# Loading two scalars first on two queues, a mask made as one minimum, and a scheduler that counts the first loads' landing

## The chip, the cores and the metric

The kernel runs on one core of one Trainium2 chip. Times are microseconds (us) of device time for one execution; the number quoted for the kernel before, 606.26 us, is the median of 3 runs (606.16 to 608.05). A core has five engines that run side by side: PE (TensorE, matrix products), DVE (VectorE), ACT (ScalarE), POOL (GpSimd) and SP (SyncE, which here only issues DMAs). Each engine executes its own instructions strictly in the order in which they were written for it. DMAs are issued from SP and from ACT; each of the two has its own DMA queue (q1 and q10 in the profile).

## The reference, cut to what matters

```python
B, H, S, D = 2, 8, 768, 64                      # attention; n_global = 8, n_local = 96 are inputs
scores = q @ k.T / sqrt(D)
keep  = (pos_k < n_global) | ((rel >= 0) & (rel < n_local))      # rel = pos_q - pos_k
dist  = where(is_global & ~is_local, n_local, abs(rel))
scores = where(keep, scores - slope[h] * dist, -1e9)
x = softmax(scores) @ v                                           # (1536, 512) over heads
x = silu(x @ w1_in) @ w1_out                                      # 512 -> 2048 -> 512
out = leaky_relu(x @ w2_in) @ w2_out                              # 512 -> 2048 -> 512
```

Only a band of 96 keys, and the first few global keys, enter a row of scores. n_global and n_local are 64-bit integers in DRAM and are known only when the kernel runs, so the mask is made on the chip.

## The kernel before, in words

**Attention.** It is cut into 24 units: two batches, three stretches of 256 queries, four pairs of heads. Unit by unit, PE transposes q and k (`pt`, line 936), ACT or DVE copies them out (`kT`, line 222 or 224, and `qT`, line 951; DVE also copies the global keys beside each block, line 948), PE makes scores (`s`, line 979), DVE adds the mask and takes the row minimum in one instruction (line 1012), ACT takes the exponential (1019), DVE divides (1035), PE transposes the result (`pa`, 1052), and PE multiplies with v (`pv`, 1078). Every unit reads the mask, first `mask0`, then `mask`.

**Mask.** `load_n` (line 77) issues two DMAs on SP that spread n_global and n_local to 128 partitions (`nraw`). DVE turns the 64-bit integers into floats (`masks_n`, 827). POOL makes the column part from n_global (`masks_global`, 834, two instructions), DVE makes the band part (`masks_local`, 838), and DVE joins them (`masks_both`, 842).

**The two layers.** The weights are read as 64-bit floats, and DVE and ACT turn them into pairs of 32-bit parts (`st`, `f`, `wi`, `wo`, lines 264 to 288). PE then does the first layer's products (`ph`, 600), the second's (`po`, 655) and, in later parts, products of sums (`pq`, 490). The products of the first layer are mixed between the units of attention: they are what PE has to do while DVE and ACT work on scores.

**Warm-up.** `warm_up` puts 27 products of zeros (`wps`, 878) into PE's order: 8 before anything else, 3 around the first two units, 16 more at a late priority.

**The order.** `Sched` (120) is a list scheduler that runs when the kernel is built. Each task has an engine, a duration, a priority and its dependences; the scheduler plays through the kernel with these durations and writes each engine's instructions in the order in which they would start. A DMA's landing is put at `max(end, dma) + 1.7` (191). The order is fixed; on the chip each engine waits at an instruction until what it needs is there. The DMAs share eight completion semaphores in turn, so the ninth DMA that is written waits, on its issuing engine, until the first has landed, the tenth until the second, and so on.

Of the kernel before, what the change touches and what calls it, by code (L numbers as in the profile page):

```python
# [9 lines left out]
F32 = mybir.dt.float32  # L10
F32R = mybir.dt.float32r
I32 = mybir.dt.int32
AF = mybir.ActivationFunctionType
ALU = mybir.AluOpType
PSUM = bass.MemoryType.PSUM

P = 128
# [4 lines left out]
BIG = float(2.0 ** 41)  # L22
# [4 lines left out]
def kernel(  # L27
# [23 lines left out]
    nc = tc.nc  # L51
# [14 lines left out]
    const = ctx.enter_context(tc.tile_pool(name="const", bufs=1))  # L66
# [4 lines left out]
    warm = const.tile([P, 1], F32, name="warm")  # L71
# [5 lines left out]
    def load_n(eng):  # L77
        for x, src in enumerate((n_global, n_local)):
            eng.dma_start(out=nraw[:, x], in_=src.bitcast(I32).partition_broadcast(P))
# [5 lines left out]
    m8nl = const.tile([P, 1], F32, name="m8nl")  # L85

# [33 lines left out]
    class Sched:  # L120
# [19 lines left out]
        def run(self):  # L140
# [3 lines left out]
            for t in self.tasks:  # L144
                for e in t["eng"]:
                    free.setdefault(e, 0.0)
                    ready.setdefault(e, [])
                for b in t["bufs"]:
                    if b.tile is not None and not b.held:
                        b.held = True  # L150
                        used[b.key] = used.get(b.key, 0) + 1
            seq, dma = 0, 0.0
# [12 lines left out]
            while len(order) < len(self.tasks):  # L165
                for e in free:
# [22 lines left out]
                    if t["dma"]:  # L189
                        dma = max(dma, now + 0.4) + t["land"]  # L190
                        end = max(end, dma) + 1.7
                    else:
                        end += t["land"]
# [591 lines left out]
    with ExitStack() as es:  # L785
# [28 lines left out]
        m8rel, pen, col = mk[:, 0:256], mk[:, 256:512], mk[:, 512:640]  # L814
        nc.gpsimd.iota(
            m8rel[:, P:256], pattern=[[8, P]], base=0, channel_multiplier=-8, allow_small_or_imprecise_dtypes=True
        )
        nc.gpsimd.affine_select(
# [5 lines left out]
        )  # L824
        nc.gpsimd.iota(col, pattern=[[1, P]], base=0, channel_multiplier=0, allow_small_or_imprecise_dtypes=True)

        def masks_n():
            nc.vector.tensor_copy(npair, nraw)
            nc.vector.tensor_scalar(nhi, npair[:, :, 0], 0.0, None, op0=ALU.is_lt)
            nc.vector.tensor_tensor(nhi, nhi, npair[:, :, 1], op=ALU.add)  # L830
            nc.vector.scalar_tensor_tensor(nf, nhi, float(2.0 ** 32), npair[:, :, 0], op0=ALU.mult, op1=ALU.add)
            nc.vector.tensor_scalar(m8nl, nlf, -8.0, None, op0=ALU.mult)

        def masks_global(eng):
            eng.tensor_scalar(col, col, ngf, -BIG, op0=ALU.is_ge, op1=ALU.mult)
            eng.tensor_scalar(col, col, m8nl, 0.0, op0=ALU.add, op1=ALU.add)

        def masks_local():
            nc.vector.tensor_scalar(pen, m8rel, m8nl, -BIG, op0=ALU.is_le, op1=ALU.mult)
            nc.vector.tensor_tensor(mask, m8rel, pen, op=ALU.add)  # L840

        def masks_both():
            nc.vector.tensor_copy(mask[:, NPV:P], col[:, 0:NG])
            nc.vector.tensor_tensor(mask0, mask[:, P:256], col, op=ALU.max)

        masks = (masks_n, masks_global, masks_local, masks_both)
# [13 lines left out]
        nload = add("SP", 0.9, lambda eng: load_n(eng), -13.0, (), (), land=0.1)  # L860
        add("ACT", 1.4, lambda eng: eng.activation(warm, warm, AF.Exp), -9.0, (), (), at=2.0)
        mt = add("DVE", 0.95, lambda eng: masks[0](), -0.5, (nload,), (), at=3.9)
        mp = add("POOL", 0.9, lambda eng: masks[1](eng), -0.5, (mt,), ())
        mt = add("DVE", 0.75, lambda eng: masks[2](), -0.5, (mt,), ())
        mtask = add("DVE", 0.45, lambda eng: masks[3](), -0.5, (mt, mp), ())
# [400 lines left out]
```

## Time and profile before

| | us |
|---|---|
| median of 3 runs | 606.26 |
| the profiled execution, its own time | 607.96 |
| its span, from the first to the last instruction | 606.2 |
| PE busy | 596.1 |
| DVE busy | 528.4 |
| ACT busy | 305.4 |

The profile tells of one execution. Its span (606.2) is what the views cut into pieces; the 1.8 us between the span and that execution's own time lie outside the views. Engine time is "busy" when an instruction stands on the engine; a line of the wait view says how long an engine sat idle and which event ended that. For DMAs the issue (how long the issuing engine is held) and the landing (from issue to the last byte's completion) are two numbers.

### The profile page before, as it was taken

The page shows a single profiled execution, that of the slowest core. Times are in us where ns is not written, and L with a number is a line of the kernel's source. Part 1 is how long each engine was busy: PE and PEld are TensorE (multiplying, and loading weights), DVE is VectorE, ACT ScalarE, POOL GpSimd, SP SyncE. Part 2 cuts the span into 40 slices and gives each one's busy share as a digit, 9 for nine tenths or more (in the row PEclk, how much of TensorE's full clock was granted, in tenths as well). Part 3 has the DMA queues.
Part 4 walks back from the last instruction along what each step waited for, and adds up shares of the span by engine and source line. Part 5 has one row for each costly group of instructions (what it writes and reads, how often), then busy time and mean ns, then how long its engine had stood idle before and what let it go on. Part 6 is the DMA issues. An engine that isn't in the chain of part 4 may idle for free.

```text
span 606.2 us, 9115 instructions
## 1 busy us (share of the span) xinstructions
PE 596.1 (98%) x3266; PEld 490.0 (81%) x3267; DVE 528.4 (87%) x1213; ACT 305.4 (50%) x682; POOL 3.7 (1%) x20
## 2 busy tenths in 40 slices
PE   8999999999999999999999999999999999999996
PEld 4678777778888888888888888898898889888985
DVE  4999999877999999995999999899999997978551
ACT  4789887876654435432555554556343433333110
POOL 2000000000000000000000000000000000000000
PEclk9999999999999999999999999999999999999999
DMA  8875568310012332322231111322132322010112
GB/s 180 185 174 141 136 167 203 71 36 1 0 36 70 105 105 69 106 69 70 69 105 35 36 35 36 105 69 85 54 105 71 104 70 69 6 65 1 70 55 90
DMA packets 72676, 49.43 MB, mean 82 GB/s; under 512 B 50480, under 2 KB 67120, under 8 KB 72624
## 3 DMA queue, kind: packets, MB, share of 16 engines
q1 hardware_dynamic: 71536, 48.51, 28.6%
q8 instruction: 28, 0.46, 0.3%
q10 hardware_dynamic: 1088, 0.26, 0.2%
q14 instruction: 24, 0.20, 0.1%
HBM read 45.62 MB, written 3.15 MB: 80 GB/s over the span
## 4 chain that ended last, share of the span: by engine, by line
PE 94%; DVE 3%; DMA 2%; ACT 1%; issue 0%; ACTq 0%
PE po L655 43%; PE pq L490 29%; PE ph L600 10%; PE s L979 3%; PE pa L1052 3%; PE pv L1078 3%; PE pt L936 2%; DMA st<-in_moe_w_in_dram 1%; DVE A L1012 1%; PE wps L878 1%; DMA q<-in_q_dram 1%; DVE A L1035 0%; DMA k<-in_k_dram 0%; ACT AT L222 0%; ACT A L1019 0%; DVE f L279 0%
## 5 line engine op out<-in xcount | busy, mean ns | idle before, releaser
L655 PE MATMUL po<-g,wo 128*128 128x512 f32 x576 | 141.5, 392 | 0.0
L655 PE MATMUL po<-wo,g 128*128 128x512 f32 (+1 forms) x588 | 136.2, 385 | 0.0
L655 PEld LDWEIGHTS po<-wo,g 128*128 128x128 f32 x588 | 107.7, 188 | 21.0
L655 PEld LDWEIGHTS po<-g,wo 128*128 128x128 f32 x576 | 106.9, 188 | 21.7 <-DVE wo L288 0.2
L600 PE MATMUL ph<-x,wi 128*128 128x512 f32 (+1 forms) x336 | 77.6, 366 | 0.9 <-DVE wi L288 0.6
L505 DVE TENSOR_TENSOR tl<-tl,pq 128x512 f32<-128x512 f32 (+1 forms) x110 | 64.3, 585 | 10.3 <-PE pq L490 5.3
L600 PEld LDWEIGHTS ph<-x,wi 128*128 128x128 f32 x336 | 56.4, 188 | 11.0 <-DVE wi L288 1.2
L490 PE MATMUL pq<-xs,ws 128*128 128x512 f32 x252 | 62.3, 389 | 0.0
L490 PEld LDWEIGHTS pq<-xs,ws 128*128 128x128 f32 x252 | 47.3, 188 | 9.8
L273 ACT ACTIVATE st<-st 128x512 f32<-128x512 f32 x64 | 42.9, 670 | 23.5 <-DMA st<-in_moe_w_out_dram 13.2
L1019 ACT ACTIVATE A<-A,nm 128x256 f32<-128x256 f32 (+1 forms) x96 | 46.1, 483 | 12.1 <-DVE nm L1012 11.9
L687 DVE SCALAR_TENSOR_TENSOR yp<-po,yp 128x512 f32<-128x512 f32 x60 | 40.7, 686 | 9.4 <-PE po L655 9.1
L279 DVE SCALAR_TENSOR_TENSOR f<-st,f 128x512 int32<-128x512 int32 x64 | 43.9, 687 | 0.9
L282 DVE SCALAR_TENSOR_TENSOR f<-st,f 128x512 int32<-128x512 int32 x64 | 43.8, 684 | 0.4
L575 ACT ACTIVATE g<-tl 128x512 fp32r<-128x512 f32 x40 | 25.0, 630 | 37.5 <-DVE tl L570 29.0
L490 PE MATMUL pq<-xn,wi 128*128 128x512 f32 (+1 forms) x192 | 43.1, 336 | 0.0
L1012 DVE CUSTOM_DVE_ANT_0 A<-s,mask 128x256 f32<-128x256 f32 (+1 forms) x96 | 34.7, 393 | 3.9 <-PE s L979 3.7
L222 ACT ACTIVATE wo<-f 128x512 fp32r<-128x512 f32 x30 | 18.9, 630 | 34.6 <-PE po L655 17.2
L490 PEld LDWEIGHTS pq<-xn,wi 128*128 128x128 f32 x192 | 32.3, 189 | 4.5
L578 DVE TENSOR_TENSOR g<-tl,g 128x512 fp32r<-128x512 f32 x40 | 27.1, 686 | 5.1 <-ACT g L575 4.8
L575 ACT ACTIVATE g<-t 128x512 fp32r<-128x512 f32 x32 | 20.1, 630 | 19.7 <-PE po L655 10.8
L276 DVE TENSOR_SCALAR f<-st 128x512 int32<-128x512 int32 x64 | 26.7, 420 | 1.6 <-ACT st L273 1.6
(119 smaller groups left out, 883.2 us busy)
## 6 DMA issues: line engine op xcount, KB each, us to landing
st<-in_moe_w_in_dram SPq DMA_DIRECT2D x32, 512.0 KB, 3.8
st<-in_moe_w_out_dram SPq DMA_DIRECT2D x32, 512.0 KB, 3.6
vd<-in_v_dram SPq DMA_DIRECT2D x24, 128.0 KB, 2.8
q<-in_q_dram SPq DMA_DIRECT2D x22, 128.0 KB, 3.1
k<-in_k_dram SPq DMA_DIRECT2D x22, 128.0 KB, 3.4
out_dram<-yo SPq DMA_DIRECT2D x11, 256.0 KB, 2.1
vp<-in_v_dram SPq DMA_DIRECT2D x20, 96.0 KB, 2.7
vp<-in_v_dram SPq DMA_DIRECT2D x20, 32.0 KB, 2.4
```

The costliest lines, as they stand in the source:

```text
L273: eng.activation(hf, hf, AF.Copy, scale=2.0 ** -112)
L279: eng.scalar_tensor_tensor(fi(), lo(), 29, fi(), op0=ALU.logical_shift_right, op1=ALU.bitwise_or)
L282: eng.scalar_tensor_tensor(fi(), hi(), -(2 ** 31), fi(), op0=ALU.bitwise_and, op1=ALU.bitwise_or)
L490: eng.matmul(bank[c]()[:, :w], wt_()[:, a, f0:f0 + P], x()[:, b, c0:c0 + w], start=(first and kk == 0 and i == 0), stop=(kk == 1 and i == ...
L505: eng.tensor_tensor(dst[0]()[:, dst[1]], a[0]()[:, a[1]], b[0]()[:, b[1]], op=op)
L575: eng.activation(g()[:, 0, :], t(), AF.Copy)
L578: eng.tensor_tensor(g()[:, 1, :], t(), g()[:, 0, :].bitcast(F32), op=ALU.subtract)
L600: eng.matmul(ph()[:, :w], wv[:, a, kk, :], xs[kk]()[:, b, cs], start=(kk == 0 and i == 0), stop=(kk == NKK - 1 and i == 2),)
L655: eng.matmul(po()[:, :w], lhsT, rhs, start=(j == 0 and i == 0), stop=(j == FPP - 1 and i == 2))
L687: eng.scalar_tensor_tensor(dst()[:, cs], po()[:, :w], scale, y()[:, cs], op0=ALU.mult, op1=ALU.add)
L1012: eng.tensor_tensor_reduce(A()[:, i, j, c0:256], s[j]()[:, i, c0:256], mask0 if c0 else mask, -QSCALE * SLOPE[2 * hp + j], 3.0e38, ALU.add ...
L1019: eng.activation(a, a, AF.Exp, bias=nm()[:, x:x + 1], scale=-1.0, accum_out=su()[:, x:x + 1])
```

## The change

Three things change. The two scalars are loaded by the first DMA of ACT's queue (n_global) and the first of SP's (n_local), ahead of all q and k; before, both stood on SP behind the first two q loads. The mask is made from tables of distances that POOL prepares without n (three new instructions on POOL, in place of the two that waited for n); what depends on n is then four DVE instructions on the tables in place of four on DVE and two on POOL, and `masks_n` keeps five. And the scheduler starts SP and ACT at 0.75, and puts a DMA's landing at the later of 2.4 after its issue and 1.7 after its turn on the DMA engines; with other numbers the whole order of the program is found anew.

```diff
-    def load_n(eng):
-        for x, src in enumerate((n_global, n_local)):
-            eng.dma_start(out=nraw[:, x], in_=src.bitcast(I32).partition_broadcast(P))
+    def load_n(eng, x):
+        eng.dma_start(out=nraw[:, x], in_=(n_global, n_local)[x].bitcast(I32).partition_broadcast(P))
...
-                    free.setdefault(e, 0.0)
+                    free.setdefault(e, 0.75 if e in ("SP", "ACT") else 0.0)
...
-                        end = max(end, dma) + 1.7
+                        end = max(end + 2.4, dma + 1.7)
...
+        nc.gpsimd.tensor_scalar(far[:, P:256], m8rel[:, P:256], BIG / 4, -BIG, op0=ALU.mult, op1=ALU.add)
...
+        nc.gpsimd.tensor_scalar(far[:, 0:P], m8rel[:, 0:P], BIG / 4, -BIG, op0=ALU.mult, op1=ALU.add)
...
+        nc.gpsimd.tensor_scalar(col, col, -2 * BIG, -BIG, op0=ALU.mult, op1=ALU.add)
...
-            nc.vector.tensor_scalar(nhi, npair[:, :, 0], 0.0, None, op0=ALU.is_lt)
-            nc.vector.tensor_tensor(nhi, nhi, npair[:, :, 1], op=ALU.add)
+            nc.vector.scalar_tensor_tensor(nhi, npair[:, :, 0], 0.0, npair[:, :, 1], op0=ALU.is_lt, op1=ALU.add)
...
-        def masks_global(eng):
-            eng.tensor_scalar(col, col, ngf, -BIG, op0=ALU.is_ge, op1=ALU.mult)
-            eng.tensor_scalar(col, col, m8nl, 0.0, op0=ALU.add, op1=ALU.add)
+            nc.vector.tensor_scalar(nfar, nf, 2 * BIG, None, op0=ALU.mult)
...
-            nc.vector.tensor_scalar(pen, m8rel, m8nl, -BIG, op0=ALU.is_le, op1=ALU.mult)
-            nc.vector.tensor_tensor(mask, m8rel, pen, op=ALU.add)
+            nc.vector.scalar_tensor_tensor(mask, far, nfar[:, 1:2], m8rel, op0=ALU.add, op1=ALU.min)
...
-        def masks_both():
+        def masks_global():
+            nc.vector.tensor_scalar(col, col, nfar[:, 0:1], m8nl, op0=ALU.add, op1=ALU.min)
+            nc.vector.tensor_tensor(mask0, mask[:, P:256], col, op=ALU.max)
             nc.vector.tensor_copy(mask[:, NPV:P], col[:, 0:NG])
-            nc.vector.tensor_tensor(mask0, mask[:, P:256], col, op=ALU.max)
...
-        nload = add("SP", 0.9, lambda eng: load_n(eng), -13.0, (), (), land=0.1)
-        add("ACT", 1.4, lambda eng: eng.activation(warm, warm, AF.Exp), -9.0, (), (), at=2.0)
-        mt = add("DVE", 0.95, lambda eng: masks[0](), -0.5, (nload,), (), at=3.9)
+        nload = [
+            add(e, 0.42, lambda eng, x=x: load_n(eng, x), -15.0, (), (), land=0.05, dma=True)
+            for x, e in enumerate(("ACT", "SP"))
+        ]
+        add("ACT", 1.4, lambda eng: eng.activation(warm, warm, AF.Exp), -9.0, (), (), at=2.7)
+        mt = add("DVE", 1.0, lambda eng: masks_n(), -5.0, nload)
```

On ACT, at the very start of the program, stand the loads of the first two units' k (`k`, two loads for each unit), the load of the table for the exponential, a dummy exponential, and the first copies. Before:

```order
L893 DMA k<-in_k_dram 128x2x64 x4
L861 ACT_TABLE_LOAD
L861 ACTIVATE warm<-warm 128x1 [waits DVE_49]
L222 ACTIVATE kT<-pt 128x2x128 [waits PE_49]
L951 ACTIVATE qT<-pt,qsc 128x256 [waits Pool_49]
```

And now (DMAHW0 is the semaphore that the load of n_global, first of all, completes):

```order
L78 DMA nraw<-in_n_global_dram 128x2
L895 DMA k<-in_k_dram 128x2x64 x3
L895 DMA k<-in_k_dram 128x2x64 [waits DMAHW0_49]
L864 ACT_TABLE_LOAD
L864 ACTIVATE warm<-warm 128x1 [waits DVE_49]
L223 ACTIVATE kT<-pt 128x2x128 [waits PE_49]
```

The load of n_global went ahead of the four k loads, and the fourth of them, and the table load behind it, now stand behind a wait for n_global. On SP it is alike: n_local is issued first, then three q loads, and the fourth q load waits for n_local's landing; before, the third q load waited for the first k load's.

On PE, after the first 8 warm-up products, stand the transposes of the first two units and their scores. Before:

```order
L936 MATMUL pt<-ident,q 128x128 x2
L936 MATMUL pt<-ident,k 128x128 x2
L936 MATMUL pt<-ident,q 128x128 x2
L936 MATMUL pt<-ident,k 128x128 x2
L878 LDWEIGHTS zero
L878 MATMUL wps<-zero 128x512
L878 LDWEIGHTS zero
L878 MATMUL wps<-zero 128x512
L878 LDWEIGHTS zero
L878 MATMUL wps<-zero 128x512
L979 MATMUL s_198<-kT,qT 128x128
```

And now:

```order
L938 MATMUL pt<-ident,q 128x128 x2
L938 MATMUL pt<-ident,k 128x128 x2
L880 LDWEIGHTS zero
L880 MATMUL wps<-zero 128x512
L880 LDWEIGHTS zero
L880 MATMUL wps<-zero 128x512
L938 MATMUL pt<-ident,q 128x128 x2
L938 MATMUL pt<-ident,k 128x128 x2
L981 MATMUL s_195<-kT,qT 128x128
```

Two of the three warm-up products moved from behind the second unit's transposes to ahead of them; the third stands now between the first unit's scores and the second's.

On PE, further on, the sixth unit's scores (`s_497` before, `s_485` now) and the first products of the first layer (`ph`). Before:

```order
L936 MATMUL pt<-ident,q 128x128 x2
L936 MATMUL pt<-ident,k 128x128 x2
L600 MATMUL ph<-x,wi 128x256 x6
L1052 MATMUL pa<-ident,A 128x128 x6
L600 MATMUL ph<-x,wi 128x256 x3
L979 MATMUL s_497<-kT,qT 128x256
```

And now:

```order
L981 MATMUL s_485<-kT,qT 128x256
L981 MATMUL s_487<-kT,qT 128x256
...
L1080 MATMUL pv<-AT,vd 64x128 x2
L1080 MATMUL pv<-AT,vp 64x128 x2
L1080 MATMUL pv<-AT,vd 64x128 x2
L938 MATMUL pt<-ident,q 128x128 x2
L938 MATMUL pt<-ident,k 128x128 x2
L601 MATMUL ph<-x,wi 128x256 x12
```

The first `ph` stood 9 ahead of the sixth unit's scores; now 12 stand behind them. Ahead of the seventh unit's scores there were 18, and are 12 now; ahead of the eighth's and the ninth's there are 30 and 54, as before.

## Rows read from the trace of the kernel before

**Rows 1.** The page's first part: busy time, share, instructions of each engine
```profile
PE 596.1 (98%) x3266; PEld 490.0 (81%) x3267; DVE 528.4 (87%) x1213; ACT 305.4 (50%) x682; POOL 3.7 (1%) x20
```

**Rows 2.** Stretches: length, busy PE, PEld, DVE, ACT, POOL, PEclk, DMA, GB/s
```profile
120.00:606.00 486.00, 480.34 (x2388) 403.33 (x2386) 422.37 (x808) 210.36 (x391) 0.00 (x0) 1.00 0.20 62
```

**Rows 3.** PE's waits in the whole span: total us, times, longest
```profile
PE wps L878 <- DVE zero L868: 1.2, 1, 1.2
PE pa L1052 <- DVE A L1035: 1.0, 2, 0.7
PE pt L936 <- DMA q<-in_q_dram: 0.7, 1, 0.7
PE ph L600 <- DVE wi L288: 0.6, 1, 0.6
PE s L979 <- ACT qT L951: 0.5, 1, 0.5
```

**Rows 4.** Timeline of PE, first 14 us: start, length, what, idle before
```profile
1.21 3.60 PE L878 MATMUL wps<-zero 128*128 128x512 bf16 x8 [1.21 <-DVE zero L868]
4.60 0.64 PE L936 MATMUL pt<-ident,q 128*128 128x128 f32 x2
...
6.35 0.79 PE L936 MATMUL pt<-ident,q 128*128 128x128 f32 x2 [0.69 <-DMA q<-in_q_dram]
...
7.36 1.49 PE L878 MATMUL wps<-zero 128*128 128x512 bf16 x3
8.77 2.31 PE L979 MATMUL s<-kT,qT 64*128 64x128 f32 x16
...
11.51 2.32 PE L878 MATMUL wps<-zero 128*128 128x512 bf16 x10
```

**Rows 5.** Timeline of DVE, 5 to 11 us
```profile
5.80 0.17 DVE L828 CAST npair<-nraw 128x4 f32<-128x4 int32 x1 [4.64 <-DMA nraw<-in_n_local_dram]
...
7.30 0.43 DVE L840 TENSOR_TENSOR mask<-mk 128x256 f32<-128x256 f32 x1
...
8.49 0.28 DVE L844 TENSOR_TENSOR mask<-mask,mk 128x128 f32<-128x128 f32 x1
8.70 0.25 DVE L948 COPY kT<-kT 128x160 f32<-128x160 f32 x1
10.46 0.29 DVE L1012 CUSTOM_DVE_ANT_0 A<-s,mask 128x128 f32<-128x128 f32 x1 [1.51 <-PE s L979]
```

**Rows 6.** Timeline of SP's DMA issues, first 4 us
```profile
1.74 0.46 SPq L79 DMA_DIRECT2D nraw<-in_n_global_dram  x1
2.24 0.43 SPq L79 DMA_DIRECT2D nraw<-in_n_local_dram  x1
3.10 1.96 SPq L893 DMA_DIRECT2D q<-in_q_dram  x4
```

**Rows 7.** Timeline of ACT, first 5 us
```profile
0.73 2.06 ACTq L893 DMA_DIRECT2D k<-in_k_dram  x4
2.82 1.28 ACT L861 ACT_TABLE_LOAD   x1 [2.82 <-issue]
```

**Rows 8.** Timeline of POOL, 7 to 9 us
```profile
7.58 0.80 POOL L836 TENSOR_SCALAR mk<-mk,m8nl 128x128 f32<-128x128 f32 x1
```

**Rows 9.** DMA issues, first 5 us: count, KB each, us from issue to landing
```profile
nraw<-in_n_global_dram SPq DMA_DIRECT2D x1, 1.0 KB, 2.7
nraw<-in_n_local_dram SPq DMA_DIRECT2D x1, 1.0 KB, 3.5
```

**Rows 10.** The chain that ended last, in order of time: start, us, what
```profile
0.73 2.35 DMA k<-in_k_dram
...
3.10 3.20 DMA q<-in_q_dram
```

**Rows 11.** DMA queues, 2.0 to 2.7 us: packets, MB, share of 16 engines
```profile
q10 hardware_dynamic: 284, 0.07, 44.2%
```

**Rows 12.** DMA queues, 3.5 to 5.2 us
```profile
q10 hardware_dynamic: 375, 0.09, 23.9%
```

More of the change, by code (lines that the diff above doesn't have):

```diff
@@ L85 @@
     m8nl = const.tile([P, 1], F32, name="m8nl")
+    nfar = const.tile([P, 2], F32, name="nfar")
     qsc = const.tile([P, NHP], F32, name="qsc")
@@ L151, in run @@
                         used[b.key] = used.get(b.key, 0) + 1
-            seq, dma = 0, 0.0
+            dma = 0.0
+            heapq.heappush(ev, (0.75, -1, 2))
             def enter(t):
@@ L813 @@
         mk = kp.tile([P, 640], F32, name="mk")
-        m8rel, pen, col = mk[:, 0:256], mk[:, 256:512], mk[:, 512:640]
+        m8rel, far, col = mk[:, 0:256], mk[:, 256:512], mk[:, 512:640]
         nc.gpsimd.iota(
@@ L824 @@
         )
+        nc.gpsimd.tensor_scalar(far[:, 0:P], m8rel[:, 0:P], BIG / 4, -BIG, op0=ALU.mult, op1=ALU.add)
         nc.gpsimd.iota(col, pattern=[[1, P]], base=0, channel_multiplier=0, allow_small_or_imprecise_dtypes=True)
+        nc.gpsimd.tensor_scalar(col, col, -2 * BIG, -BIG, op0=ALU.mult, op1=ALU.add)
         def masks_n():
             nc.vector.tensor_copy(npair, nraw)
-            nc.vector.tensor_scalar(nhi, npair[:, :, 0], 0.0, None, op0=ALU.is_lt)
-            nc.vector.tensor_tensor(nhi, nhi, npair[:, :, 1], op=ALU.add)
+            nc.vector.scalar_tensor_tensor(nhi, npair[:, :, 0], 0.0, npair[:, :, 1], op0=ALU.is_lt, op1=ALU.add)
             nc.vector.scalar_tensor_tensor(nf, nhi, float(2.0 ** 32), npair[:, :, 0], op0=ALU.mult, op1=ALU.add)
             nc.vector.tensor_scalar(m8nl, nlf, -8.0, None, op0=ALU.mult)
-        def masks_global(eng):
-            eng.tensor_scalar(col, col, ngf, -BIG, op0=ALU.is_ge, op1=ALU.mult)
-            eng.tensor_scalar(col, col, m8nl, 0.0, op0=ALU.add, op1=ALU.add)
+            nc.vector.tensor_scalar(nfar, nf, 2 * BIG, None, op0=ALU.mult)
         def masks_local():
-            nc.vector.tensor_scalar(pen, m8rel, m8nl, -BIG, op0=ALU.is_le, op1=ALU.mult)
-            nc.vector.tensor_tensor(mask, m8rel, pen, op=ALU.add)
-        def masks_both():
+            nc.vector.scalar_tensor_tensor(mask, far, nfar[:, 1:2], m8rel, op0=ALU.add, op1=ALU.min)
+        def masks_global():
+            nc.vector.tensor_scalar(col, col, nfar[:, 0:1], m8nl, op0=ALU.add, op1=ALU.min)
+            nc.vector.tensor_tensor(mask0, mask[:, P:256], col, op=ALU.max)
             nc.vector.tensor_copy(mask[:, NPV:P], col[:, 0:NG])
-            nc.vector.tensor_tensor(mask0, mask[:, P:256], col, op=ALU.max)
-        masks = (masks_n, masks_global, masks_local, masks_both)
         sc = Sched(dict(SIZES, pt=2, s=4, q=2, k=2, vd=2, vp=2, nm=4, su=4, rs=4))
@@ L858 @@
         kT, kdone = {}, {}
-        nload = add("SP", 0.9, lambda eng: load_n(eng), -13.0, (), (), land=0.1)
-        add("ACT", 1.4, lambda eng: eng.activation(warm, warm, AF.Exp), -9.0, (), (), at=2.0)
-        mt = add("DVE", 0.95, lambda eng: masks[0](), -0.5, (nload,), (), at=3.9)
-        mp = add("POOL", 0.9, lambda eng: masks[1](eng), -0.5, (mt,), ())
-        mt = add("DVE", 0.75, lambda eng: masks[2](), -0.5, (mt,), ())
-        mtask = add("DVE", 0.45, lambda eng: masks[3](), -0.5, (mt, mp), ())
+        nload = [
[4 more added lines that the diff above has]
+        mt = add("DVE", 1.0, lambda eng: masks_n(), -5.0, nload)
+        mt = add("DVE", 0.43, lambda eng: masks_local(), -2.0, (mt,))
+        mtask = add("DVE", 0.6, lambda eng: masks_global(), -2.0, (mt,))
         add("DVE", 0.6, lambda eng: flags(), 20.0, (mtask,), at=20.0)
```

## The prediction

> **What bounds the kernel now.** I read the page's first part, then the stretches, then PE's waits, then the first 14 us engine by engine. PE is busy 596.1 of 606.2 us [rows 1], so at most 10.1 us can be won by taking idle time from PE. From 120 us to the end PE lacks 486.0 - 480.3 = 5.7 us [rows 2]; the waits list no stall of PE there, and the 5.7 us are the tail (last sum, last store), whose order is the same in both programs. That leaves 10.1 - 5.7 = 4.4 us of idle PE ahead of 120 us, and the waits name 4.0 of them: 1.2 until the zeros are written, 1.0 and 0.5 in the chain of attention, 0.7 for the second unit's q, 0.6 for the first weights [rows 3]. Beside this stand the 27 warm-up products, which fill time in which PE had nothing to do. So the change can only win or lose at the head, where work for PE is not yet there; further on PE has enough waiting for it (all its idle time but the tail lies ahead of 120 us), an order found anew costs nothing there, and what the head wins or loses arrives at the end one for one.
>
> At the head the reader is to see which engine waits for what. PE is in its first 8 warm-up products until 4.60, transposes the first unit, waits 0.69 us for the second unit's q, transposes it, does 3 warm-up products, and starts the scores at 8.77 [rows 4]. DVE begins on n at 5.80 and has the mask at 8.49 + 0.28 = 8.77; the first use of the mask is at 10.46, and it waited 1.51 us for PE's scores, not for the mask [rows 5]. So the mask is not on the path: an earlier mask alone is worth nothing. What sets the start of DVE's long row of work is the first unit's scores on PE, and these stood behind 1.49 us of warm-up products [rows 4], which stood behind the second q.
>
> **The change part by part.**
>
> *The mask's instructions.* Nine on DVE remain: five small ones (about 0.2 us apart, from the first at 5.80), one at 0.43, and three of which the nearest row is 0.28 [rows 5]: about 1.0 + 0.43 + 0.75 = 2.2 us. They run while DVE has nothing else, ahead of the scores; cost 0. The cover ends if n lands so late that landing + 2.2 us passes the first scores (about 10 us), that is if n landed after 7.8. POOL gains three instructions of up to 0.80 each [rows 8], 2.4 us, from about 2.5 us on, done by about 5.5; DVE needs them at landing + 1.0. If POOL is last there, DVE waits up to 1 us under the same cover; cost 0.
>
> *When n lands.* Before, the two loads were issued at 1.74 and 2.24 [rows 6] and took 2.7 and 3.5 us [rows 9], landing at 4.44 and 5.74. Now both are issued at about 0.73, where each queue's first load was [rows 7]. If they don't hinder each other they land at 0.73 + 2.7 = 3.4; if they go one after the other, the pair takes 5.74 - 1.74 = 4.0 and the later lands at 4.7. I take 4.2.
>
> *What stands behind n.* The ninth and tenth loads, the last k and the last q of the second unit, wait on ACT and SP until n has landed. Issued at 4.2 (3.4 to 4.7) and landing 2.35 to 3.20 us later, as the loads of 64 KB in [rows 10], they are there at 6.8 (5.8 to 7.9); before, the q that PE waited for landed at 6.30. Behind ACT's waiting load stand the table load, 1.28 us [rows 7], then the dummy exponential and the first unit's copies: table done at 4.2 + 0.5 + 1.3 = 6.0 (at most 6.5), where the first copy is wanted when PE's first transposes end, about 6.2. So it is just covered; at worst 0.3 us late, and the scores have slack for that. Behind SP's waiting load stand all later loads of q, k, v and weights: SP is at its fifth q load at 4.7, before at 4.0, so they are up to 0.7 us later; none of PE's first waits but the named one is for a load, so I take 0 for this.
>
> *The first transposes.* Every load of the first unit is issued one load later (0.46 us [rows 6]) and stands in its queue behind n. Before, they had landed well ahead of 4.60, when PE left the warm-up products. The range is 4.60 (hidden) to 5.7 (one us after n's late landing). I take 5.1.
>
> *The moved warm-up products.* First unit's transposes from 5.1 for 1.0 us (7.36 - 6.35 for the second's before); two products at 3.60 / 8 = 0.45 [rows 4], to 7.0; second unit's transposes from 7.0, their last load being there at 6.8, for 1.0; and the scores at 8.0 at once instead of 8.77. Gain 0.8. Best case: transposes at 4.60, scores at 7.5, gain 1.3. Worst of these bounds: last load at 7.9, half of the second transposes behind it, scores at 8.4, gain 0.4. The first use of the mask follows the scores' start by 10.46 - 8.77 = 1.69 us, so DVE starts on them at 9.7, with the mask done by 6.4 to 7.0 and the second copy of keys (0.25 [rows 5]) ahead of 9.
>
> *The new order behind that.* The first `ph` come 12 behind the sixth unit's scores instead of 9 ahead of them. PE no longer stands in front of weights that are not ready (0.6 in [rows 3]) with the sixth unit's scores behind it; the attention chain runs on, and some of the 1.0 for `pa` goes too. Against it, for one more unit PE has no filler: up to 9 `ph`, about 1.0 us, are done later in DVE's shadow. By the eighth unit both orders have done 30. Bounds: gain 1.2, loss 1.0. I take a gain of 0.3, the nearest to the middle that leaves out half the wait for the weights.
>
> *Sum:* 0.8 + 0.3 = 1.1 us less. Against the profiled execution's own 607.96 us (span 606.2 and 1.8 outside) that is 606.9; the median of the runs shown is 606.26, 1.7 below that execution, and I forecast for a median: 606.26 - 1.1 = 605.2 us.
>
> **A rule weighed against the trace.** From 2.0 to 2.7 us, before the packets of n, ACT's queue moved 284 packets in 0.7 us, 406 a us; from 3.5 to 5.2, while n's two loads were under way on SP's queue, it moved 375 in 1.7 us, 221 a us [rows 11, 12]: a load of n on one queue goes with a slower other queue. The Trainium skill (page "Trainium Kernel Development and Optimization", section Key Constraints) says that DMAs from SP, ACT and POOL all run on the same 16 DMA engines and interleave, so that issuing from several saves only the issue time. The trace agrees as far as it goes. By that rule the two loads of n don't run side by side, n lands at the late end, 4.7, and the gain at the scores would be 0.4 instead of 0.8; the sum above stands on the rows' bounds.
>
> **The rivals.** A gain or loss under 0.3%, 1.8 us, can't be told from no change here; the runs before alone spread over 1.9.
>
> *A: PE's pace rises earlier.* The first 8 warm-up products took 0.45 us each, the ten from 11.51 took 0.23 [rows 4]: half pace, that is TensorE's level of 1.2 GHz, and full pace, 2.4 GHz (the granted clock in the stretches reads 1.00 throughout, so only the durations show it). At the start of the program PE has one gap, 0.69 us. With two warm-up products in that place the gap shrinks or goes. If PE then reaches full pace before the second unit's transposes, these (1.0) and the scores up to the first mask (1.69) take half: 1.3 us more won, 0.8 + 1.3 + 0.3 = 2.4, giving 603.9. Against it: the gap may only move ahead of the first transposes (4.6 to 5.1).
>
> *B, slower: n chokes both queues.* Place: the first microseconds of both DMA queues; price: everything of the first two units behind it. If the two loads, side by side with each other and ahead of 16 engines' worth of q and k, land no earlier than before, at 5.7, the ninth and tenth loads are issued then and land 3.2 later, at 8.9; the scores start at 9.4 instead of 8.8, 0.6 lost. PE then stands idle for about 1.9 us (7.0 to 8.9) instead of 0.69, and if its full pace comes as long after that idle time as before (6.35 to the midst of the scores, about 10, since 16 products there took 2.31), it comes at 12.5: up to 2.5 us at half pace, 1.3 lost. Together 1.9: 608.2. It decides from the point where n lands later than about 5.1 (last load at 8.3, scores at 8.8: no longer earlier). For it: the slower queue in [rows 12], and that each of n's loads kept its queue 1.3 us (4.44 to 5.74). Against: with two queues each has only one.
>
> *C: nothing is won, the first loads come no earlier.* The change names n as first, and q and k pay for it: if the first transposes start at 5.7, the scores start at 5.7 + 1.0 + 0.9 + 1.0 = 8.6, and the 0.2 left and the new order behind come out at nothing: 606.3.
>
> **How the numbers follow.** Forecast 0.58, A 0.20, B 0.10, C 0.12. Faster by over 0.3% (below 604.4): A, and the best end of the forecast's terms (1.3 + 1.2 = 2.5), 0.04: together 0.24. Slower by over 0.3% (above 608.1): B, 0.10. The rest, 0.66, within. The range takes A's time and the best end of the forecast's terms at the lower end (603.6), and at the upper end C's time with the spread upwards that the runs before show (1.8 over their lowest), short of B: 607.8.
>
> **What would show it.** Right: n's first conversion on DVE starts at 4 to 5 us and the mask is ready near 7; the fourth k and q loads are issued at n's landing; the scores start near 8.0 and the first use of the mask near 9.7 with the releaser still PE; PE's wait for `wi` is gone. A shows as warm-up products at 0.23 us before 9 us. B shows as `pt` waiting over 1 us for q or k, and a first use of the mask after 11. The prediction is wrong if PE's idle time ahead of 120 us changes by much without any of these, in the units 5 to 9, where the new order has 6 `ph` fewer ahead of the seventh unit's scores.

## The result, and the profile after

The changed kernel takes 609.32 us (median of 6 runs, 608.59 to 610.25); before, on the same chip, 606.21 (6 runs, 605.58 to 608.05). The ratio is 1.0051, with an interval of 1.0039 to 1.0063: slower by 3.1 us, more than the 0.3% that can be told from no change, where 605.2 was forecast. Its profiled execution took 608.59 us, of which the span is 606.8.

The first part of its page, busy time, share and instructions of each engine:

```profile
PE 595.0 (98%) x3267; PEld 488.2 (80%) x3267; DVE 529.0 (87%) x1214; ACT 303.5 (50%) x681; POOL 3.0 (1%) x21
```

Beside [rows 1] TensorE (PE) does the same work in 1.1 us less and has 606.8 - 595.0 = 11.8 us of idle time, where before it had 10.1. The head, which the prediction watched, looks like a success. DMA issues of the first 12 us (count, KB each, us to landing), then rows of the timelines of VectorE (DVE), ScalarE (ACT), SyncE (SP) and PE (start, length, what, idle before it and its releaser):

```profile
nraw<-in_n_global_dram ACTq DMA_DIRECT2D x1, 1.0 KB, 4.1
nraw<-in_n_local_dram SPq DMA_DIRECT2D x1, 1.0 KB, 3.8
```

```profile
4.86 0.17 DVE L834 CAST npair<-nraw 128x4 f32<-128x4 int32 x1 [3.69 <-DMA nraw<-in_n_global_dram]
...
6.79 0.17 DVE L846 COPY mask<-mk 128x32 f32<-128x32 f32 x1
...
8.40 0.29 DVE L1014 CUSTOM_DVE_ANT_0 A<-s,mask 128x128 f32<-128x128 f32 x1 [0.41 <-PE s L981]
```

```profile
5.26 1.28 ACT L864 ACT_TABLE_LOAD   x1 [5.26 <-DMA nraw<-in_n_global_dram]
```

```profile
1.20 5.14 SPq L895 DMA_DIRECT2D q<-in_q_dram  x6
```

```profile
1.23 3.60 PE L880 MATMUL wps<-zero 128*128 128x512 bf16 x8 [1.23 <-DVE zero L870]
5.30 0.70 PE L938 MATMUL pt<-ident,q 128*128 128x128 f32 x2 [0.48 <-DMA q<-in_q_dram]
...
6.11 0.59 PE L880 MATMUL wps<-zero 128*128 128x512 bf16 x2
...
7.45 0.93 PE L981 MATMUL s<-kT,qT 64*128 64x128 f32 x8 [0.16 <-ACT qT L953]
```

Against [rows 9] each length takes longer, against [rows 5] the mask is done 1.8 us earlier, at 6.96, and its first use comes at 8.40 in place of 10.46. The two warm-up products at 6.11 took 0.59 us together, 0.30 each, where the first eight took 0.45: PE passes from half pace to full about there, and in the trace of before only at about 10 [rows 4]. So that trace, from which the sum was made, is of an execution that came to full pace late. In e4 below, with before's order and loads, it comes at about 6.5: the moment is not a property of the order alone.

The loss stands further on. Busy time by stretches (length, PE, PEld, DVE, ACT, POOL, PEclk, DMA share, GB/s), first of before, then of the changed kernel:

```profile
10.00:25.00 15.00, 14.46 (x119) 9.46 (x118) 13.73 (x65) 11.60 (x42) 0.00 (x0) 1.00 0.84 196
25.00:60.00 35.00, 33.44 (x291) 27.40 (x291) 34.28 (x128) 31.10 (x96) 0.00 (x0) 1.00 0.67 168
34.00:60.00 26.00, 25.77 (x232) 21.46 (x232) 25.50 (x91) 22.98 (x71) 0.00 (x0) 1.00 0.63 164
```

```profile
10.00:25.00 15.00, 13.85 (x114) 9.09 (x111) 12.04 (x63) 12.29 (x46) 0.00 (x0) 1.00 0.97 216
25.00:60.00 35.00, 32.20 (x283) 26.22 (x283) 34.40 (x122) 28.84 (x89) 0.00 (x0) 1.00 0.67 166
34.00:60.00 26.00, 23.89 (x210) 19.92 (x210) 25.44 (x91) 21.48 (x67) 0.00 (x0) 1.00 0.61 160
```

From 25 to 60 us DVE is full in both programs (34.3 and 34.4 of 35). From 34 to 60 us PE lacks 2.1 us, before 0.2. From 10 to 25 us DVE does 1.7 us less, but this pair of traces is not like for like: before's starts late, and up to 25 us DVE has been busy for 16.3 us in the changed kernel (4.28 ahead of 10 us) and 16.4 in before (2.69). The head start was gone by then. A fair pair, e3 and e4, both early, stands below. The changed kernel's waits of PE in that stretch (in total, times, longest; before's trace has none there) name DVE each time:

```profile
PE pa L1054 <- DVE x L1095: 0.9, 1, 0.9
PE pa L1054 <- DVE A L1037: 0.9, 3, 0.5
PE ph L601 <- DVE wi L289: 0.3, 1, 0.3
```

What DVE does later in the changed kernel is the conversion of the first weights. ACT's first step of it (`st`) and DVE's first two (`f`), before and after:

```profile
15.23 0.67 ACT L273 ACTIVATE st<-st 128x512 f32<-128x512 f32 x1
...
19.62 0.41 DVE L276 TENSOR_SCALAR f<-st 128x512 int32<-128x512 int32 x1
20.06 0.69 DVE L279 SCALAR_TENSOR_TENSOR f<-st,f 128x512 int32<-128x512 int32 x1
```

```profile
22.65 0.67 ACT L274 ACTIVATE st<-st 128x512 f32<-128x512 f32 x1
...
18.11 0.29 DVE L1014 CUSTOM_DVE_ANT_0 A<-s,mask 128x128 f32<-128x128 f32 x1 [0.89 <-PE s L981]
...
22.23 0.42 DVE L1014 CUSTOM_DVE_ANT_0 A<-s,mask 128x256 f32<-128x256 f32 x1 [0.71 <-PE s L981]
...
23.35 0.43 DVE L277 TENSOR_SCALAR f<-st 128x512 int32<-128x512 int32 x1 [0.19 <-ACT st L274]
```

The weights were issued at 10.65 before and at 11.80 after, 1.2 us later, but ACT takes them up 7.4 us later: the planner has put `st` behind another unit's work. At 18 and 22 us, where before did `f`, DVE now stands for PE's scores. This follows from the order, and so the first question was which edit brings the order in.

### The profile page after: what moved, and what is told of

It is laid out like the page before. It is cut to its first block, busy times and chain, and to the rows that moved or that the text cites. A ratio compares the mean times of both kernels' runs of the same rounds, so it can differ in the third digit from the quotient of the medians.

```text
span 606.8 us, 9129 instructions
## 1 busy us (share of the span) xinstructions
PE 595.0 (98%) x3267; PEld 488.2 (80%) x3267; DVE 529.0 (87%) x1214; ACT 303.5 (50%) x681; POOL 3.0 (1%) x21
## 4 chain that ended last, share of the span: by engine, by line
PE 91%; DVE 5%; DMA 1%; ACT 1%; issue 0%; SPq 0%; DVEq 0%
PE po L656 43%; PE pq L491 29%; PE ph L601 10%; PE s L981 3%; PE pv L1080 3%; PE pa L1054 2%; PE pt L938 1%; DVE A L1037 1%; DVE A L1014 1%; DMA nraw<-in_n_global_dram 1%; PE wps L880 1%; DMA vp<-in_v_dram 1%; ACT A L1021 1%; DVE f L283 0%; DVE f L280 0%; DVE AT L225 0%
## 5 line engine op out<-in xcount | busy, mean ns | idle before, releaser
L1054 PE MATMUL pa<-ident,A 128*128 128x128 f32 x176 | 26.5, 277 | 3.0 <-DVE A L1037 2.0
```

The lines of the kernel that those rows point to most:

```text
L1054: eng.transpose(pa()[:, j, c, :], A()[:, i, j, c * P:(c + 1) * P], ident)
```

## The experiments

In what follows Theory 1 is that the weights' later place on DVE is the loss; 1b, that any newly found order loses; 2, that the lengths in front hold up the other loads; 3, that the moment of PE's full pace decides. Interval means that of the ratio to before, which ran beside each kernel.

**e1_head**: before's order, the new mask, the lengths first.

```diff
         with tc.manual_schedule(engines={E.PE, E.DVE, E.Activation, E.SP, E.Pool}):
+            load_n(nc.scalar, 0)
+            load_n(nc.sync, 1)
             sc.run()
```


> The order of the kernel before on every engine, but n_global and n_local are the first loads on ACT and SP, and the mask is made in the new way. Theory 1 (the new order costs: the weights' conversion stands one unit later on DVE, which idles about 2 us more between 10 and 25 us): 605.0 to 606.7, no slower than before. Theory 2 (the loads of n in front cost: q and k queue behind them and the table load waits for n): 608 to 609.5, as the changed kernel. Theory 3 (nothing but the moment at which PE reaches full pace differs): 606 or 608, by chance, with runs in two groups some 1.8 us apart.

**e2_n_behind**: the changed kernel with the lengths behind the first two q on SP.

```diff
-            add(e, 0.42, lambda eng, x=x: load_n(eng, x), -15.0, (), (), land=0.05, dma=True)
+            add(e, 0.42, lambda eng: None, -15.0, (), (), land=0.05, dma=True)
...
+                    if m == 0 and h == 0 and ts[0][1] is q:
+                        load_n(eng, 0)
+                        load_n(eng, 1)
```


> The order of the changed kernel, with its scheduler's numbers and new mask, but both loads of n stand on SP behind the first two q loads, as before. Theory 1: 608 to 609.5, as slow as the changed kernel, DVE idle about 3 us between 10 and 25 us. Theory 2: 606 to 607, the loss is gone. Theory 3: two groups of runs.

**e3_start075**: before with one number of the planner changed.

```diff
-                    free.setdefault(e, 0.0)
+                    free.setdefault(e, 0.75 if e in ("SP", "ACT") else 0.0)
...
```
The line left out lets the planner wake up at 0.75.

> The kernel before with one number of the scheduler changed: SP and ACT start at 0.75 in its model; n and mask as before. The first layer's products then stand as in the changed kernel (0 ahead of the sixth unit's scores, 12 ahead of the seventh's). Theory 1: 608 to 609.5, all of the loss without any change to n or mask. Theory 2: 606.2. Theory 3: 606 or 608.

**e4_mask**: before with the new mask alone.

```diff
-            nc.vector.tensor_scalar(pen, m8rel, m8nl, -BIG, op0=ALU.is_le, op1=ALU.mult)
-            nc.vector.tensor_tensor(mask, m8rel, pen, op=ALU.add)
+            nc.vector.scalar_tensor_tensor(mask, far, nfar[:, 1:2], m8rel, op0=ALU.add, op1=ALU.min)
...
```


> The kernel before, its order and its loads, with the mask made in the new way. Theories 1 and 2: 606.2 within 0.5, since DVE waited for scores and not for the mask. Theory 3: runs in two groups; a profile from the lower group would show PE's full pace before the first scores (warm-up products of 0.23 us before 9 us) and the third unit's scores near 14.0 instead of 15.8.

Measured, beside 606.77 of before: e1 607.92 (interval 1.0005 to 1.0033), e2 609.15 (1.0022 to 1.0044), e3 609.19 (1.0026 to 1.0046), e4 606.51 (0.9981 to 1.0007). The mask costs and gains nothing. One number in the planner, with no load and no instruction changed, costs 2.4 us, most of the 3.1. Its trace from 34 to 60 us has the changed kernel's row almost to the hundredth, and e4's is close to before's; first e3, then e4:

```profile
10.00:25.00 15.00, 13.61 (x112) 8.94 (x111) 12.34 (x65) 12.49 (x47) 0.00 (x0) 1.00 0.87 203
25.00:60.00 35.00, 32.22 (x281) 26.37 (x281) 34.45 (x120) 28.74 (x90) 0.00 (x0) 1.00 0.68 166
34.00:60.00 26.00, 23.90 (x209) 20.04 (x207) 25.48 (x90) 21.40 (x68) 0.00 (x0) 1.00 0.64 162
```

```profile
10.00:25.00 15.00, 13.74 (x109) 8.97 (x109) 14.16 (x63) 12.37 (x44) 0.00 (x0) 1.00 0.95 210
25.00:60.00 35.00, 34.19 (x307) 28.46 (x306) 34.58 (x129) 31.65 (x96) 0.00 (x0) 1.00 0.66 163
34.00:60.00 26.00, 25.91 (x233) 21.94 (x230) 25.68 (x91) 23.48 (x71) 0.00 (x0) 1.00 0.60 153
```

Both executions come to full pace by 7 us, so this pair is like for like. With the new order DVE does 1.8 us less from 10 to 25 us, is as full as in e4 from 25 to 60, and PE does 2.0 us less there. Their spans are 607.0 and 603.8 us, 3.2 apart, of which 2.3 are idle time of PE (12.1 against 9.8). These are single executions, and e4's is the fastest of its ten; but by them the order alone can be worth all of the 3.1. Before's 31 runs reach from 605.8 to 608.5, e3's ten only from 608.8 to 609.7; that late executions among before's raise its median, and so bring the difference of the medians down to 2.4, fits this and is not shown. e2, e3 and e4 came out where Theory 1 put them, e1 between the theories.

The lengths in front cost 1.4 us in before's order (e1 against e4). In the new order no cost shows (609.3 against e2's 609.15, on different chips), but the two intervals, 1.0039 to 1.0063 and 1.0022 to 1.0044, do not exclude one of about 1 us.

**e5_after_w30, e6_after_w25, e7_before_w40**: the due time of the first weights in the planner, 3.5 in both kernels, moved to 3.0 and to 2.5 in the changed kernel, to 4.0 in before.

```diff
-                return 3.5 + 1.2 * j if which == "in" else 8.0 + 1.3 * j
+                return 3.0 + 1.2 * j if which == "in" else 8.0 + 1.3 * j
```
The other two have 2.5 and 4.0 in that line.

> The changed kernel with one number more changed: the due time of the first part's first weights is 3.0 instead of 3.5, so that DVE finishes the first converted weights at the fifth unit's first mask (as in the kernel before) and 9 products of the first layer stand ahead of the sixth unit's scores, 21 ahead of the seventh's. Theory 1 (the loss comes from the weights' place on DVE): 606 to 607, with DVE idle about 1 us between 10 and 25 us instead of 3.0. Theory 1b (any order found anew loses against the one before, wherever the weights stand): 608.5 to 610, DVE idle alike. Theory 2 (n in front): 608 to 609.5.

> The same with 2.5: the weights stand one unit earlier still (15 products ahead of the sixth unit's scores, 24 ahead of the seventh's). Theory 1: 605 to 607, DVE not idle more than 1 us between 10 and 25 us. Theory 1b: 608.5 to 610. If DVE waits for weights that have not landed, it shows as DVE or ACT waiting for the DMA of the weights before 20 us, and the time is above e5's.

> The kernel before with that due time at 4.0 instead of 3.5 and nothing else: the first products stand as in the changed kernel (0 ahead of the sixth unit's scores, 12 ahead of the seventh's, then 27 and 45). Theory 1: 608.5 to 610, DVE idle about 3 us between 10 and 25 us. Theory 2: 606.5, since n and mask are as before. Theory 1b: 608 to 610 too, so this run speaks only between 1 and 2.

Measured, beside 606.73: 608.4 (1.0013 to 1.0032), 610.39 (1.0032 to 1.0065), 613.02 (1.0062 to 1.0102). None of the three falls into the range that Theory 1 gave it. Later weights are worse, as expected, and by more; in part this is TensorE's clock. PE stood 1.65 us for A until 35.78, and behind that the granted clock fell, which it did in neither e3 nor e4 (length, PE, PEld, DVE, ACT, POOL, PEclk, DMA, GB/s):

```profile
36.00:42.00 6.00, 5.80 (x34) 4.88 (x33) 4.54 (x16) 2.81 (x9) 0.00 (x0) 0.72 0.54 146
```

Earlier weights give back something at 3.0 and lose at 2.5, where PE's idle time from 34 to 60 us is 2.2 us: the place alone does not settle it.

**e8_gap**: e4 with two of the three warm-up products between the first two units' transposes, as the changed order has them.

```diff
+                if n == 0:
+                    warm_up(2)(eng)
...
-                add("PE", 0.5, warm_up(2 - u["n"]), -3.0, (u["T"],), (wps,))
+                add("PE", 0.5, warm_up(u["n"]), -3.0, (u["T"],), (wps,))
```


> The order of the kernel before with the new mask and n at its old place, as e4, but two of the three warm-up products stand between the first and the second unit's transposes, where PE sat idle 0.69 us. Theory 3 (the moment of PE's full pace makes the two groups of runs, and the idle time there decides it): all runs in the lower group, 605.6 to 606.4, no run above 607.5. If the idle time has no part in it: the same spread as the kernel before, 605.8 to 608.5.

Measured: 607.05 (0.9986 to 1.0015; runs from 606.3 to 609.4). A miss for Theory 3; the spread is that of before. It was no clean test: in its one trace full pace comes at about 4.4 us, ahead of the moved products, and PE still stands 0.97 us for the second unit's q, so the idle time was not closed but grew.

**e9_landing24**: before with only the landing number of the change.

```diff
-                        end = max(end, dma) + 1.7
+                        end = max(end + 2.4, dma + 1.7)
```


> Before with only the landing number of the change in the planner (2.4 for the least time of a transfer), the loads and the mask as before. The order found has 6, 18, 30, 54 and 81 first-layer matmuls ahead of the scores of units 6 to 10, before's has 9, 18, 30, 54 and 81, that of the change 0, 12, 30, 54 and 84. Theory 1 (what costs is that the weights' conversions stand a unit later on VectorE): 606.4 to 607.3 us, idle of VectorE at 10 to 25 us as before (13.5 to 14.2 busy), TensorE over 25.5 of 26 us busy at 34 to 60 us. Theory 1b (any order found anew is worse than the one that the kernel was tuned with): 608.5 or more.

**e10_w30_n_behind**: e2 with the due time 3.0 of e5.

```diff
-                return 3.5 + 1.2 * j if which == "in" else 8.0 + 1.3 * j
+                return 3.0 + 1.2 * j if which == "in" else 8.0 + 1.3 * j
```


> The changed kernel with the first weights due at 3.0 in place of 3.5, and the lengths loaded behind the first two loads of q as before. Theory 1 with Theory 3 (e5_after_w30 lost because its TensorE came to full pace only at 10 us, which the lengths in front bring about by the gap ahead of the first transposes): no wait for q at 4.8 us, full pace by 7 us in the profile, 606.3 to 607.5 us. Theory 1b: 608 to 609, as e5.

**e11_head_warm9**: e1 with one more product in PE's gap.

```diff
-        add("PE", 3.4, warm_up(8), -9.0, (), (wps,), at=1.2)
+        add("PE", 3.4, warm_up(9), -9.0, (), (wps,), at=1.2)
```


> e1_head with nine warm-up matmuls in place of eight ahead of the first transposes, which fill TensorE's 0.48 us of waiting for q there; nothing else. Theory 3 (the lengths in front cost by that gap, after which TensorE stays at half pace until 10 us): 606.0 to 607.0 us, runs below 606.5 among them, full pace by 7 us. Theory 2 (the lengths in front delay the loads of q and k themselves): 607.5 to 608.5, like e1.

**e12_n_on_pool**: e1 with the lengths on GpSimd's (POOL's) queue.

```diff
-            load_n(nc.scalar, 0)
-            load_n(nc.sync, 1)
+            load_n(nc.gpsimd, 0)
+            load_n(nc.gpsimd, 1)
```


> Before's order and the new mask, the lengths loaded first on GpSimd's queue, so that SyncE and ScalarE issue q and k at once, and nothing stands behind the lengths. Theory 2 and Theory 3 agree that the first transposes start at 4.6 us or earlier, and the second pair's wait for q of 0.7 us gets shorter by up to 0.7, since two issues of 0.4 us are gone from SyncE: 605.5 to 606.5 us, beside 606.7 of before. If GpSimd's loads land later than 8 us, the mask is late for its first use at 10.4 us, and it is 607 or more.

Measured, beside 606.52:

- e9 608.06 (1.0010 to 1.0029), between the two theories. DVE is busy for 14.21 us from 10 to 25 us, as in e4, but PE stands 1.10 us for A ahead of 24.94, and from 25 to 30 us the granted clock is 0.66.
- e10 607.81 (1.0009 to 1.0026), also between its two ranges: 1.3 less than e2, so over half of what the new order lost comes back with the weights' place, and 1.3 beside before does not.
- e11 607.53 (1.0003 to 1.0024), hardly better than e1, as Theory 2 expected and Theory 3 did not.
- e12 610.36 (1.0046 to 1.0080), spoilt, since the loads were issued behind POOL's iotas and DVE stood for them until 8.42. PE then stood 2.54 us for a copy of k, and the granted clock from 10 to 15 us was 0.69.

In e11 the gap on PE is filled, and the trace (SP's issues, then ACT, then PE) shows what the lengths cost besides:

```profile
1.19 5.17 SPq L892 DMA_DIRECT2D q<-in_q_dram  x6
...
11.86 0.51 SPq L264 DMA_DIRECT2D st<-in_moe_w_in_dram  x1
```

```profile
17.03 0.68 ACT L273 ACTIVATE st<-st 128x512 f32<-128x512 f32 x1 [2.94 <-DMA st<-in_moe_w_in_dram]
```

```profile
18.77 0.49 PE L978 MATMUL s<-kT,qT 64*128 64x128 f32 x4 [1.02 <-ACT qT L950]
```

SP waits 1.9 us for a length to land among its six q, and reaches the first weights at 11.86, in e4 at 10.67; ACT, whose order has `st` next, stands 2.94 us for them (1.98 in e4), and PE 1.02 for the `qT` behind it (0.45 in e4). In e1's trace, which is late, these two waits are 1.92 and 0.45, as in e4: there the lost time does not show at this place.

**e13_cut_new_order, e14_cut_old_order**: one of DVE's five operations left out of the first four pieces of weights, in e2 and, as control, in e4; no place in the order moves.

```diff
             def op_c(eng):
+                if which == "in" and L == 0 and fc < 4:
+                    return
```


> e2_n_behind with one of VectorE's five operations left out of the conversion of the first four pieces of the first layer's weights (their lowest mantissa bits are lost): 4 operations of about 0.62 us, 2.5 us of VectorE's time between 20 and 55 us, with no change in the order. Theory 1 (in the new order VectorE's work of that stretch is what TensorE waits for): the idle of TensorE at 34 to 60 us falls from 2.1 us to under 0.8, and the time from 609.15 to 606.8 to 607.8. Theory 1b (the order itself, by TensorE's own places, loses the time wherever VectorE stands): 608.5 or more.

> The control to e13_cut_new_order: the same four operations left out of e4_mask, whose order is that of before. Theory 1: TensorE idles only 0.1 to 0.2 us at 34 to 60 us there, so there is little to win: 606.0 to 606.7 us beside 606.5. If it gains as much as e13_cut_new_order does against e2_n_behind (2 us, 604.5 or less), the cut is worth the same in either order and Theory 1 falls.

**e15_pool_first**: e12 with the loads ahead of the iotas.

```diff
+        load_n(nc.gpsimd, 0)
+        load_n(nc.gpsimd, 1)
         m8rel, far, col = mk[:, 0:256], mk[:, 256:512], mk[:, 512:640]
```


> e12_n_on_pool with the two loads of the lengths ahead of GpSimd's iotas, not behind them: before's order, the new mask, SyncE and ScalarE free for q and k from the start. e12 issued them at 4.9 us, and VectorE, which waits for them ahead of the copies of k, stood until 8.4. Theory 2 (the lengths in front of q and k on their queues cost about 1 us, as in e1 and e11): both lengths land by 6 us, VectorE is not later than in e4_mask (5.85), the second q pair is transposed at 5.5 in place of 6.4, and the time is 605.3 to 606.4 us. If they land at 7 us or later it is 608 or more again.

Measured, beside 606.7: e13 608.19 (1.0013 to 1.0031), e14 606.6 (0.9995 to 1.0017), e15 606.38 (0.9985 to 1.0002; all 11 runs from 606.02 to 606.98). The cut is worth 1.0 us in the new order and nothing in the old: DVE's load does hold up PE in the new one, for some 1 us and not for 2, so e13 falls between the two ranges it was given. Its trace is of its slowest run, 610.54, where the others reach from 607.8 to 608.6: PE stood 2.04 us for `x` until 56.97, and from 55 to 60 us the granted clock was 0.71. With before's order and mask kept, taking the lengths off SP and ACT makes e1's 607.92 into 606.38 (their runs of before took 606.77 and 606.7): Theory 2, with a price of 1.5.

In e15's trace PE, after its warm-up, gets the second unit's q without a wait and stands for the copy of k instead, behind the mask on DVE:

```profile
5.35 0.70 PE L937 MATMUL pt<-ident,q 128*128 128x128 f32 x2
...
8.18 1.53 PE L980 MATMUL s<-kT,qT 64*128 64x256 f32 x12 [0.77 <-DVE kT L949]
```

**e16_after_cut**: the same cut in the changed kernel.

```diff
             def op_c(eng):
+                if which == "in" and L == 0 and fc < 4:
+                    return
```


> The changed kernel itself with the four operations of e13_cut_new_order left out (the lowest mantissa bits of four pieces of weights are lost), so that the trace of e13, whose profiled run was 2 us slower than its others, can be read beside another. Theory 1 in the size that e13 gave it: about 1 us faster than the changed kernel's 609.3, 608.0 to 608.6; at 34 to 60 us the waits for A (0.9 us) and wi (0.3 us) are gone or nearly so, and the wait for x (0.9 us) stays. If the wait for x goes too, the time is 607.5 or less and all of the loss was VectorE's load.

**e17_pool_before_all**: e15 with the loads ahead of POOL's other constants too.

```diff
+    load_n(nc.gpsimd, 0)
+    load_n(nc.gpsimd, 1)
+
     npair = const.tile([P, 2, 2], F32, name="npair")
```


> e15_pool_first with the two loads of the lengths ahead of all of GpSimd's constants but the identity's, so that they are issued at about 1 and 1.7 us in place of 1.9 and 3.0. By e15's trace the lengths land 3.3 us after the issue, at about 5.0, VectorE's mask starts 1.5 us earlier and the 0.8 us that TensorE waits for the copy of k at 7.4 to 8.2 goes: 605.5 to 606.2 us, beside 606.4 of e15 and 606.7 of before. If VectorE then waits for k instead, it is as e15.

Measured for the last two, beside 606.97: e16 609.42 (7 runs, three from 607.8 to 608.1 and four from 609.4 to 611.3; 1.0022 to 1.0054), no gain in the median over the 609.3 of the changed kernel, and a miss for the expected 608.0 to 608.6. Beside the runs of before that went with each, it is 2.45 us slower against 3.1, with intervals that overlap, so e16 neither confirms nor refutes the 1 us of e13. Its trace, a run with full pace at 10 us where the changed kernel's comes at 6, shows which waits go and which stays. PE's waits in e16 from 34 to 60 us:

```profile
PE pa L1056 <- DVE x L1097: 1.2, 1, 1.2
PE pa L1056 <- DVE A L1039: 0.2, 1, 0.2
```

Without the four operations the waits for A (0.9) and `wi` (0.3) shrink to 0.2, and the one for `x` stays. It even grows, since ACT, which makes the first half of `x`, stands 0.96 us for a load of second-layer weights just ahead of it (1.80 in e13). What the wait for `x` is, the traces show without a further run. First the changed kernel, DVE then PE, and then the same place in e4, DVE then PE:

```profile
55.14 1.14 DVE L1037 TENSOR_SCALAR A<-A,rs 128x256 f32<-128x256 f32 x4
56.19 0.41 DVE L1095 TENSOR_TENSOR x<-pv,x 128x256 fp32r<-128x256 f32 x1
56.66 1.09 PE L1054 MATMUL pa<-ident,A 128*128 128x128 f32 x8 [0.91 <-DVE x L1095]
```

```profile
53.61 1.14 DVE L1035 TENSOR_SCALAR A<-A,rs 128x256 f32<-128x256 f32 x4
54.66 0.42 DVE L1093 TENSOR_TENSOR x<-pv,x 128x256 fp32r<-128x256 f32 x1
54.09 1.29 PE L1052 MATMUL pa<-ident,A 128*128 128x128 f32 x8
```

DVE does the same two things at the same speed, but in e4 `pa` starts 0.48 us behind the start of A's division and 0.57 ahead of `x`, and in the changed kernel it starts when `x` is done. Before and e15 are as e4 here, e2 and e3 as the changed kernel. So this wait belongs to the places in the new order and not to DVE's load. The kernel takes the buffers of `pa` and of `pv`, which `x` reads, from one pool, so the new order may give `pa` the buffer that `x` still needs; that it does isn't shown.

e17 took 606.34 (0.9981 to 0.9998), just above the expected 605.5 to 606.2, and the only interval of these that lies below 1, by 0.1%. Its trace answers its expectation in part: npair starts 0.4 us earlier, at 6.11 (6.51 in e15), where 1.5 was expected, and PE waits 0.46 us for the copy of k (0.77). The loads were issued at 1.29 and 2.35, later than hoped.

## Why the prediction was wrong

**The step that failed** is "an order found anew costs nothing there", and with it the term "The new order behind that", a gain of 0.3 with a bound of 1.0 for a loss. With nothing else changed the order cost 2.4 us (e3). The step looked at PE alone: PE has other work waiting, so a shift of the first `ph` seemed to be made up by the eighth unit. The count was right, and DVE was overlooked: it is full from 25 to 60 us (34.28 of 35 before), so what it does not do from 10 to 25 us (12.34 in e3, 14.16 in e4) it can't make up. The prediction's last sentence named the place, idle PE in the units 5 to 9, but gave it no price. How the 2.4 us divide: about 1 is DVE's load (e13 against e14; the waits for A and `wi`, 1.2), which e16 did not confirm in its median; the wait of `pa` for `x`, 0.9, goes with the new places of `pa` and `x`, as the traces show, but no experiment took it away, so that it makes up the rest fits the numbers and isn't shown. Neither theory holds alone: Theory 1 expected 606 to 607 from e5 and got 608.4, and 1b expected 608.5 or more from e9 and 608 to 609 from e10 and got 608.06 and 607.81.

**"What stands behind n"**: n landed at 4.84, a little past the late end of the bounds (4.7), so as late as "one after the other" and more: 4.1 and 3.8 us on two queues, where 2.7 and 3.5 had been read. Why is not shown. The slower queue of [rows 12] does not show it: between the two windows weighed, from 2.7 to 3.5 us, with both loads of n already issued, ACT's queue moved 340 packets, 425 a us, no fewer than ahead of that. The prediction saw that SP would run late, put it at up to 0.7 and took 0, since before's waits name one load alone. SP was 1.3 us late (its six q are issued at 6.34, before at 5.06 [rows 6]), and in before's order the lengths in front cost 1.5 us (e1 against e15). Of these 1.2 are left in e11 (607.53), whose trace shows the wait for late weights and no gap, and 0.4 went when the gap did; that the 0.4 are the pace is argued, not shown. In the new order no cost was measured, and it fits that there ACT takes the weights up at 22.65, 6 us after they landed (issued at 11.80, 4.8 to landing): a delay hidden by a worse one.

**"The first transposes" and "The moved warm-up products"**: 5.30 for 5.1, and scores at 7.45 for 8.0. The direction was right, but the better number came with rival A, pace at about 6 us, and not by the sum. A's sign came true in the profiled run, and the kernel was slower all the same. So "what the head wins or loses arrives at the end one for one" failed too: the first use of the mask came 2.1 us earlier (8.40 for 10.46), and by 25 us DVE had done no more than before (16.3 and 16.4).

**Right**: the mask on DVE and POOL costs nothing (e4); POOL's three new instructions took 0.30 each where up to 0.80 was allowed; PE's stall for the second q is gone (0.69), though one of 0.48 stands now ahead of the first unit's; the stretch from 120 us on is as before (PE lacks 486.8 - 481.0 = 5.8 us, 5.7 before). **Rival B** had the right sign by the wrong place: the lengths did hold up the loads behind them, but n landed at 4.84, short of the 5.1 it set, and its place was the first two units, and they were early.

**The base**: the sum went from one execution, 607.96, at a late pace, and was then carried to the median, 606.26. Like for like at an early pace (e4's span 603.8 against 606.8) the change costs 3.0. The lower end of the range, 603.6, does not follow from the terms named for it, which give 603.8 and 603.9; the result lay beyond the other end.

## What to carry to other kernels

When a change makes a planner find a new order, look for the engine that is full behind the place where the orders part, and count what that engine does less of before it; that the engine which bounds the kernel has work waiting says nothing about this. Test the order alone first: a kernel with one number of the planner changed and nothing else gave most of the answer here in one run. And put a tiny load that others must wait for on a queue that has nothing else to issue: ahead of the large loads it cost 1.5 and 1.2 us here (e1 and e11 against e15). There it must stand ahead of that engine's own work: behind it, the same loads cost 4 us (e12 against e15).

## What the runs showed of the hardware

PE's full pace, 0.2 us for a warm-up product where half pace takes 0.45, came at moments from 4.4 us (e8, whose first transposes are short already) to 10 us (before, e1, e5), with the granted clock at 1.00 in every stretch of the head; only the products' durations show it. Before's 31 runs beside e1 reach from 605.8 to 608.5. e15, whose PE has no gap from 1.24 to 7.4 us, kept its 11 runs within 1.0 us, but e17, which has none either, spread over 1.9, and e8 and e11, which closed or moved one gap, over 3.1 and 1.8. What fixes the moment stays open.

The granted clock fell in four traces, each time behind idle time of PE in the midst of its work: to 0.66 from 25 to 30 us in e9 (1.10 us idle), 0.69 from 10 to 15 in e12 (2.54), 0.72 from 36 to 42 in e7 (1.65) and 0.71 from 55 to 60 in e13 (2.04). In e9 the eight scores of a unit took 2.08 us there and 1.13 elsewhere. It stayed at 1.00 behind the 0.91 us of the changed kernel and the 1.23 of e16.

Two loads of 1 KB, first on two queues at once, took 4.1 and 3.8 us; on POOL's queue, beside the same loads of q and k, 3.2 and 3.4 in e15 and 3.0 and 3.7 in e17.
